# Theta's weights loaded between the first head pairs, values in 128-row transfers, later float64 weights split by Prelu

## The chip, the cores and the metric

The kernel runs on one core of one Trainium2 chip. The metric is the time of one execution in microseconds (us). The core's engines are TensorE (PE in the profile; PEld is its weight load), VectorE (DVE), ScalarE (ACT), GpSimd (POOL), and SyncE (SP), which issues nearly all of the transfers.

## The reference

Three stages follow each other, for 4 batches of 576 positions: an attention with 8 heads of 64 (heads 0 to 3 look back over a window of 32, heads 4 to 7 over 32 positions with a step of 4), a mixing layer whose angles are `theta`, and a gated layer. Cut to its core:

```python
# attention: q, k, v are (4, 8, 576, 64)
scores = np.where(masks, scale * q @ k.T, -1e9)
attn = exp(scores - max); attn = attn / (sum + 1e-9)
x = attn @ v                                  # -> (4, 576, 512)
# mixing
theta = x @ w_theta                           # 512 x 512
zr, zi = x * cos(theta), x * sin(theta)
u = x + w_tok_r @ zr + w_tok_i @ zi           # over the positions, 576 x 576
x = u + relu(u @ w_ch)
# gated layer
h = relu(x @ w_in); u, v = h[..., :512], h[..., 512:]
v_s = w_spatial @ norm(v) + b_spatial
out = (u * v_s) @ w_out
```

`w_theta`, `w_tok_r`, `w_tok_i`, `w_ch`, `w_in` and `w_out` come as float64, all other inputs as float32.

## The kernel before

Every product behind the attention is done three times, with each factor split into a high part that fits TensorE's float32r and a low rest: high by high, low by high, high by low (L367, L438, L445, L464). So each weight is split once: a copy to the high part (L146, helper `copy` at L107 to L113) and a subtraction for the low part (L147).

**Pieces of float64 weights.** A weight is loaded as pairs of 32-bit words, 128 rows by 256 or 288 columns at a time; here this is called a piece. `bits64` (L117) makes float32 of it: the high word is scaled (L131 on ACT or L133 on POOL, which shifts its exponent to where float32 has it), the low word is shifted on DVE (L134), and two more DVE instructions put the two together (L135, L136). The piece then goes through `copy` and the subtraction. Which engines do the copy, the subtraction and the scaling is given by strings: `TOK_ENG` for the token weights (the two halves of their columns), `CH_ENG`, `IN_ENG`, `OUT_ENG`, and `THETA_ENG`; their letters are the engine of the high copy, of the subtraction and of the scaling (v DVE, g POOL, a ACT; without a third letter POOL). There are 8 pieces of `w_theta` (`wth` in the profile), 9 of each half of `w_tok` (`w`), 8 of `w_ch`, 16 of `w_in` and 8 of `w_out`. The landing buffers of later pieces are four (`w64`, L123), as are those of the scaled words (`w64g`, L127), so the fifth piece is loaded when the first has been read.

**The head of the program.** `attention(0)` (L517) runs batch 0: four head pairs of three groups each, twelve groups `m`. A group is scores on PE (`s`, L258, with the mask added by L253), a maximum on DVE, three exponentials on ACT (L274), a sum and a reciprocal on DVE (L275, L276), a product on POOL (`sm`, L277); two groups later transposes (`pt`, L287) and four later the product with the values (`ps_x`, L301, L305), whose results ACT copies into `x`. All loads of batch 0 are issued at its start (`att_load`): keys `kt`, queries `qz`, values `vt`, the values of a pair behind the next pair's keys and queries. The values are 96 rows (`KW`) of 4,608 bytes for each head pair.

**Theta's weights.** `w_theta_job` is called at group `TH_FROM + TH_RATE * i // 10`, so at groups 6, 6, 7, 7, 8, 9, 9, 10, and what it issues, its load included, stands behind the softmax of that group. The token weights' first half (`tok0`) stands behind the last group's softmax.

**Theta's stage.** `th_run(0, (4, 0, 1, 2, 3))` works on five units of 128 positions (unit 4 has 64): `xh` on ACT (L359), `xl` on DVE (L362), twelve matmuls on PE (`ps_th`, L367), then on ACT `ta` (L375), an absolute value (L381) and two Sines (L384, L385), with a subtraction on DVE between (L376). Products with the transposed `x` give `zz` or `spare` (L388 to L396), which are split into `zh` and `zl` (L111, L113, L339). The token sums `ps_y` (L438, L445) take the `z` tiles in the order 8, 0, 4, 1, 5, 2, 6, 3, 7, with batch 1's attention between.

The order on each engine is the scheduler's: within what the dependencies and `issue_after` allow, it orders the instructions by its own estimate of time.

```python
w_theta_job(k, c)   # L162: load, scaling, three DVE instructions, copy and subtraction on POOL
spread(th_run(0, (4, 0, 1, 2, 3)), (jobs([lambda k=k: tok0(k) for k in K_ALL]), 2.0))
```

## Time and profile before

| | |
|---|---|
| Median of 3 runs | 549.74 us (546.46 to 550.3) |
| The profiled execution | 546.96 us, span 545.1 us |
| PE busy in the span | 526.1 us (96%) |
| DVE busy | 315.0 us (58%) |
| ACT busy | 246.7 us (45%) |
| POOL busy | 261.6 us (48%) |
| PE's part of the chain that ended last | 76% |

The span runs from the first to the last instruction of the profiled execution. A busy share is an average over stages with different limits; a stage is read from its own stretch. PE's matmuls are pipelined and overlap, so its busy time counts the union of their spans.

### The profile page before, as it was taken

To read this page: it belongs to the slowest core of one execution; us is meant where nothing else is said; L and a number is where in the kernel's file an instruction comes from. 1 tells how busy PE (TensorE), PEld (TensorE's weight loads), DVE (VectorE), ACT (ScalarE), POOL (GpSimd) and SP (SyncE) were. 2 spreads that over 40 slices of the span, in tenths; PEclk is the share of its full clock that TensorE was granted. 3 is DMA by queue.
4 is the path that set the end of the run, shared out by engine and by line. 5 is a ranking of instruction groups with operands and counts; after the bars stand their busy time and mean duration, and the time that the engine had idled before them with its cause. 6 is when DMAs were issued, how large, how long until landed. Compare 5 with 4: busy or idle time off the path is not lost.

```text
span 545.1 us, 10626 instructions
## 1 busy us (share of the span) xinstructions
PE 526.1 (96%) x3860; PEld 482.4 (88%) x3860; DVE 315.0 (58%) x830; ACT 246.7 (45%) x722; POOL 261.6 (48%) x336
## 2 busy tenths in 40 slices
PE   5987999999999999999999999999999999999997
PEld 5864889988999989998889999999899889988996
DVE  2688999899778378653882145795503057253020
ACT  4949766625656444872551125543322233233221
POOL 3484896554995259720296338355303114322040
PEclk9989899999999999999999999999999999999999
...
GB/s 205 294 88 109 234 180 191 198 193 64 141 215 228 125 182 103 209 91 1 1 1 253 365 199 275 1 158 95 49 29 174 58 40 1 0 2 77 1 1 96
DMA packets 60972, 67.19 MB, mean 123 GB/s; under 512 B 23028, under 2 KB 45816, under 8 KB 60920
## 3 DMA queue, kind: packets, MB, share of 16 engines
...
q10 hardware_dynamic: 2224, 0.55, 0.5%
...
## 4 chain that ended last, share of the span: by engine, by line
PE 76%; DVE 9%; POOL 5%; issue 4%; ACT 3%; DMA 2%; ACTq 0%; POOLq 0%; DVEq 0%
PE ps_y L445 17%; PE ps_sp L725 9%; PE ps_hu L706 9%; PE ps_o L754 9%; PE ps_hv L661 9%; PE s L258 5%; PE ps_r L464 5%; PE ps_th L367 3%; PE pt L287 3%; PE ps_x L301 2%; POOL zl L339 2%; DVE xl L362 1%; PE ps_x L305 1%; PE ps_y L438 1%; DMA x2d<-parts 1%
## 5 line engine op out<-in xcount | busy, mean ns | idle before, releaser
L445 PE MATMUL ps_y<-wtok_h,zh 128*128 128x288 f32 x270 | 81.2, 304 | 1.1 <-DVE sm L270 0.7
L445 PE MATMUL ps_y<-wtok_h,zl 128*128 128x288 f32 x270 | 80.0, 298 | 0.7 <-POOL zl L339 0.7
L445 PE MATMUL ps_y<-wtok_l,zh 128*128 128x288 f32 x270 | 79.5, 298 | 0.0
L339 POOL TENSOR_TENSOR gl<-hu,gh 128x288 fp32r<-128x288 f32 x32 | 26.1, 815 | 64.5 <-ACT gh L109 64.5
L445 PEld LDWEIGHTS ps_y<-wtok_h,zh 128*128 128x128 f32 x270 | 50.4, 188 | 2.5 <-DVE sm L270 1.4
L445 PEld LDWEIGHTS ps_y<-wtok_h,zl 128*128 128x128 f32 x270 | 50.7, 188 | 1.0 <-POOL zl L339 0.9
L445 PEld LDWEIGHTS ps_y<-wtok_l,zh 128*128 128x128 f32 x270 | 50.4, 188 | 0.3
L729 DVE TENSOR_TENSOR hu<-ps_sp,hu 128x288 f32<-128x288 f32 x32 | 14.6, 455 | 61.8 <-PE ps_sp L728 61.7
L277 POOL TENSOR_TENSOR sm<-sm,l 128x288 f32<-128x288 f32 x48 | 31.9, 669 | 34.7 <-DVE l L276 19.5
L339 POOL TENSOR_TENSOR vl<-hv,vh 128x512 fp32r<-128x512 f32 x16 | 21.1, 1319 | 56.5 <-ACT vh L109 51.5
L274 ACT ACTIVATE sm<-sm,m 128x96 f32<-128x96 f32 x108 | 39.2, 365 | 10.1 <-DVE m L271 7.2
L448 DVE TENSOR_TENSOR x<-ps_y,x 128x288 f32<-128x288 f32 x40 | 17.6, 452 | 38.2 <-PE ps_y L445 37.8
L339 POOL TENSOR_TENSOR ul<-x,uh 128x288 fp32r<-128x288 f32 x32 | 26.8, 845 | 26.0 <-ACT uh L109 23.7
L725 PE MATMUL ps_sp<-wsp_h,vh 128*128 128x288 f32 x128 | 37.8, 296 | 0.0
L464 PE MATMUL ps_r<-uh,wch_h 128*128 128x288 f32 x128 | 37.6, 298 | 0.2 <-DVE x L448 0.2
L725 PE MATMUL ps_sp<-wsp_h,vl 128*128 128x288 f32 x128 | 37.7, 295 | 0.0
L725 PE MATMUL ps_sp<-wsp_l,vh 128*128 128x288 f32 x128 | 37.7, 295 | 0.0
L464 PE MATMUL ps_r<-uh,wch_l 128*128 128x288 f32 x128 | 37.7, 296 | 0.0
L706 PE MATMUL ps_hu<-x2l,win_h 128*128 128x288 f32 x128 | 37.7, 295 | 0.0
L706 PE MATMUL ps_hu<-x2h,win_h 128*128 128x288 f32 x128 | 37.7, 294 | 0.0
L706 PE MATMUL ps_hu<-x2h,win_l 128*128 128x288 f32 x128 | 37.7, 294 | 0.0
L464 PE MATMUL ps_r<-ul,wch_h 128*128 128x288 f32 x128 | 36.9, 295 | 0.0
...
## 6 DMA issues: line engine op xcount, KB each, us to landing
...
```

What stands on the lines that cost most here:

```text
L258: PE.matmul(s[:, KW * blk:KW * (blk + 1)], qz[:, t].rearrange("p j q -> p (j q)"), kt[:, T * t:T * t + KW], start=not on_pe, stop=not on_pe)
L274: ia = A.activation(sm[:, t, :], src[:, t, :], AF.Exp, bias=m_[:, t:t + 1], scale=scale, accum_out=ls[:, t, 0:1])
L277: ig = G.tensor_tensor(sm, sm, l.unsqueeze(2).to_broadcast([P, 3, KW]), op=ALU.mult)
L287: PE.transpose(pt[:KW, P * t:P * (t + 1)], sm[:, t, :], ident)
L339: return (G if el == "g" else V).tensor_tensor(dst_l, src, f32(dst_h), op=ALU.subtract)
L445: PE.matmul(ps[:, :CH], lh[b, k][:, P * d:P * (d + 1)], rh[:, k, cs], start=(n == 0), stop=(n == 3 * len(ks) - 1))
L448: V.tensor_tensor(xv, ps[:, :CH], xv, op=ALU.add)
L464: PE.matmul(ps[:, :CH], lh[:, k, P * e:P * (e + 1)], rh[:, k, cs], start=(n == 0), stop=(n == 11))
L661: PE.matmul(ps, lh[:, k, ts_], rh[:, k, DM:], start=(n == 0), stop=(n == 11))
L706: PE.matmul(ps[:, :CH], lh[:, k, fs], rh[:, k, cs], start=(n == 0), stop=(n == 11))
L725: PE.matmul(ps[:, :CH], lh[b, k][:, fs], rh[:, k, cs], start=(n == 0), stop=False)
L754: PE.matmul(ps, lh[:, k, ts_], rh[:, k, cs], start=(n == 0), stop=(n == 11))
```

## The change

Five things are changed.

1. Theta's weights are loaded by `w_theta_load` out of `att_load`: two of the eight transfers behind the values of each head pair, ahead of the next pair's keys and queries. `w_theta_job` keeps the rest.
2. The splitting of theta's eight pieces stands behind the softmax of groups 2, 3, 4, 5, 6, 7, 8 and 9.
3. Values are loaded as 128 rows: the 96 rows of a head pair and the 32 that follow them in memory (the matmuls use the first 96), 589,824 bytes instead of 442,368. The last head pair of all has no rows behind it and keeps 96.
4. Pieces that ACT scales use Prelu with a slope of 2^32 on the negative side, which leaves the sign where the last combining instruction would have put it: two DVE instructions instead of three. That holds for the token, channel, input and output weights; theta's pieces keep three.
5. The scaling of the second half of the token weights and of `w_in` goes from POOL to ACT: 9 + 16 = 25 pieces.

```diff
-TH_FROM, TH_RATE = 6, 6
+TH_FROM = (2, 3, 4, 5, 6, 7, 8, 9)
-IN_ENG, SP_ENG, OUT_ENG = "vgg", "ag", "aga"
-TOK_ENG = ("aga", "gv")
+IN_ENG, SP_ENG, OUT_ENG = "vga", "ag", "aga"
+TOK_ENG = ("aga", "gva")
...
-        last_dma[0] = SY.dma_start(st[:p, :2 * n], src.bitcast(U32))
+        if src is not None:
+            last_dma[0] = SY.dma_start(st[:p, :2 * n], src.bitcast(U32))
...
         if eng == "a":
-            A.mul(g, hw.bitcast(F32), 2.0**-112)
-        else:
-            G.tensor_scalar(g, hw.bitcast(F32), 2.0**-56, 2.0**-56, op0=ALU.mult, op1=ALU.mult)
+            A.activation(g, hw.bitcast(F32), AF.Prelu, scale=2.0**-112, alpha=2.0**32)
+            V.tensor_scalar(c, lw, 29, None, op0=ALU.logical_shift_right)
+            V.scalar_tensor_tensor(gi, gi, 3, c, op0=ALU.logical_shift_left, op1=ALU.bitwise_or)
+            return g
+        G.tensor_scalar(g, hw.bitcast(F32), 2.0**-56, 2.0**-56, op0=ALU.mult, op1=ALU.mult)
         V.tensor_scalar(c, lw, 29, None, op0=ALU.logical_shift_right)
         V.scalar_tensor_tensor(c, gi, 3, c, op0=ALU.logical_shift_left, op1=ALU.bitwise_or)
         V.scalar_tensor_tensor(gi, gi, 0x80000000, c, op0=ALU.bitwise_and, op1=ALU.bitwise_or)
...
+    def w_theta_load(k, c):
+        wth[k, c] = pz.tile([P, DM], U32, tag=f"z{'hl'[c]}{k}", name="wth64")
+        SY.dma_start(wth[k, c], w_theta[:, k, DM // 2 * c:DM // 2 * (c + 1)].bitcast(U32))
...
+    def load_v(vt, b, hp):
+
+        r = KW * (4 * b + hp)
+        n = min(P, KW * 4 * B - r)
+        SY.dma_start(vt[:n], v_rows[r:r + n])
...
         if hp:
-            SY.dma_start(heads[0, hp - 1][2], vw[0, hp - 1])
+            load_v(heads[0, hp - 1][2], 0, hp - 1)
+            for c in range(2):
+                w_theta_load(hp - 1, c)
         if hp == 3:
-            SY.dma_start(vt, vw[0, 3])
+            load_v(vt, 0, 3)
+            for c in range(2):
+                w_theta_load(3, c)
...
-            if m == TH_FROM + TH_RATE * i // 10:
+            if m == TH_FROM[i]:
```

In the built programs the change also moves instructions. The line numbers of the changed kernel are higher; its L297, L136, L150, L132, L379, L382, L395, L396, L408 and L415 are L277, L133, L147, L131, L359, L362, L375, L376, L388 and L395 of the kernel before.

POOL, at the end of batch 0's attention, before. `sm` is the softmax product, here those of the last two groups; the others split theta's weights:

```order
L277 TENSOR_TENSOR sm<-sm,l 128x288
L133 TENSOR_SCALAR w64g<-wth_416 128x256
L147 TENSOR_TENSOR wth_l<-w64g,wth_h 128x256
L113 TENSOR_SCALAR wth_h<-w64g 128x256
L277 TENSOR_TENSOR sm<-sm,l 128x288
L133 TENSOR_SCALAR w64g<-wth_456 128x256
L147 TENSOR_TENSOR wth_l<-w64g,wth_h 128x256
L113 TENSOR_SCALAR wth_h<-w64g 128x256 x2
L133 TENSOR_SCALAR w64g<-wth_465 128x256
L147 TENSOR_TENSOR wth_l<-w64g,wth_h 128x256 x2
L113 TENSOR_SCALAR wth_h<-w64g 128x256
L133 TENSOR_SCALAR w64g<-wth_497 128x256
```

Nine theta instructions stand behind the last `sm` in these rows, and five more follow them before the first subtraction of a token piece. In the changed kernel the same place reads:

```order
L297 TENSOR_TENSOR sm<-sm,l 128x288
L150 TENSOR_TENSOR wth_l<-w64g,wth_h 128x256
L136 TENSOR_SCALAR w64g<-wth_160 128x256
L113 TENSOR_SCALAR wth_h<-w64g 128x256
L136 TENSOR_SCALAR w64g<-wth_162 128x256
L297 TENSOR_TENSOR sm<-sm,l 128x288
L150 TENSOR_TENSOR wth_l<-w64g,wth_h 128x256
L113 TENSOR_SCALAR wth_h<-w64g 128x256
L150 TENSOR_TENSOR wth_l<-w64g,wth_h 128x256
L113 TENSOR_SCALAR wth_h<-w64g 128x256
L150 TENSOR_TENSOR wth_l<-w64g,wth_h 128x256
L150 TENSOR_TENSOR wtok_l<-w64g,wtok_h 128x288 x9
```

Now five theta instructions stand behind the last `sm`, and all nine subtractions of the token weights' first half follow as a block; behind that block come the first `zl`.

ACT, at the start of theta's stage, before: the first two `xh` are those of units 4 and 0, the two that follow those of units 1 and 2; `w64g<-w` is the scaling of a token piece and `wtok_h` its high copy:

```order
L359 ACTIVATE xh<-x_148 128x4x64
L359 ACTIVATE xh<-x_148 128x512
L131 ACTIVATE w64g<-w_625 128x288
L131 ACTIVATE w64g<-w_634 128x288
L131 ACTIVATE w64g<-w_681 128x288
L131 ACTIVATE w64g<-w_690 128x288
L109 CAST wtok_h<-w64g 128x288
L375 ACTIVATE ta<-ps_th,magic 64x512
L359 ACTIVATE xh<-x_148 128x512
L375 ACTIVATE spare<-ps_th,magic 128x512
L359 ACTIVATE xh<-x_148 128x512
```

In the changed kernel three scalings and a cast already stand ahead of these rows, between the last copies into `x`:

```order
L132 ACTIVATE w64g<-w_687 128x288
L379 ACTIVATE xh<-x_164 128x4x64
L379 ACTIVATE xh<-x_164 128x512
L109 CAST wtok_h<-w64g 128x288
L132 ACTIVATE w64g<-w_732 128x288
L109 CAST wtok_h<-w64g 128x288
L132 ACTIVATE w64g<-w_740 128x288
L109 CAST wtok_h<-w64g 128x288
L132 ACTIVATE w64g<-w_787 128x288
L109 CAST wtok_h<-w64g 128x288
L132 ACTIVATE w64g<-w_795 128x288
L395 ACTIVATE ta<-ps_th,magic 64x512
```

Eight scalings instead of four stand ahead of unit 4's `ta` now, and four copies instead of one stand between the second `xh` and it.

DVE, where unit 3's `xl` stands, before: `zz` are unit 4's products, `spare` those of units 0 and 1, and the row with `ps_th` is unit 1's subtraction:

```order
L395 TENSOR_TENSOR zz<-ps_xn,tb 64x512
L396 TENSOR_TENSOR zz<-ps_xn,ta 64x512
L136 SCALAR_TENSOR_TENSOR w64g<-w64g,c_100 128x288
L388 TENSOR_TENSOR spare<-ps_xn,spare 128x512 x2
L134 TENSOR_SCALAR c_100<-w_736 128x288
L376 SCALAR_TENSOR_TENSOR spare<-spare,ps_th 128x512
L111 CAST zh_672<-spare 128x512
L362 SCALAR_TENSOR_TENSOR xl<-x_148,xh 128x512
```

And in the changed kernel:

```order
L415 TENSOR_TENSOR zz<-ps_xn,tb 64x512
L416 TENSOR_TENSOR zz<-ps_xn,ta 64x512
L396 SCALAR_TENSOR_TENSOR spare<-spare,ps_th 128x512
L382 SCALAR_TENSOR_TENSOR xl<-x_164,xh 128x512
L408 TENSOR_TENSOR spare<-ps_xn,spare 128x512 x2
L111 CAST zh_670<-spare 128x512
```

Unit 3's `xl` moved ahead of unit 0's products and cast, and no piece of the token weights stands there any more. On PE the twelve matmuls of unit 4 stood between those of unit 0; now they stand in a block, but for one. The number of ACT's table loads is nine in both programs.

## Rows read from the trace of the kernel before

**Rows 1.** Stretches (us from the start): length, busy time and instructions by engine, granted clock, DMA.

```profile
core 0: us, PE busy (x) PEld busy (x) DVE busy (x) ACT busy (x) POOL busy (x), PEclk, DMA share, GB/s
28.10:34.46 6.36, 4.11 (x60) 3.17 (x59) 5.33 (x15) 3.73 (x12) 6.36 (x14) 0.86 0.38 138
42.29:50.40 8.11, 6.21 (x25) 4.43 (x24) 6.40 (x13) 8.08 (x15) 1.91 (x2) 1.00 0.39 112
50.40:59.50 9.10, 6.16 (x23) 4.62 (x24) 9.07 (x16) 7.38 (x15) 7.88 (x8) 0.84 0.66 172
59.50:290.00 230.50, 228.05 (x1905) 210.54 (x1904) 173.80 (x450) 126.31 (x396) 143.38 (x186) 1.00 0.47 135
```

**Rows 2.** Waits of PE: for whom, us in total, times, longest.

```profile
PE ps_th L367 <- ACT xh L359: 2.4, 3, 1.1
PE ps_th L367 <- DVE xl L362: 2.4, 2, 2.1
PE pt L287 <- POOL sm L277: 2.2, 2, 1.6
```

**Rows 3.** Stretches in which values, then theta's and token pieces move.

```profile
19.50:22.00 2.50, 2.50 (x25) 2.45 (x25) 2.10 (x7) 2.34 (x13) 0.67 (x1) 1.00 1.00 237
...
24.40:29.00 4.60, 4.09 (x62) 2.79 (x60) 4.50 (x16) 4.15 (x20) 4.40 (x10) 1.00 1.06 389
```

**Rows 4.** Timeline: start us, duration us, engine, line, instruction; pair 3.

```profile
10.44 0.43 SPq L216 DMA_DIRECT2D kt<-kT  x1
...
22.44 0.21 ACT L267 ACTIVATE m<-m 128x3 f32<-128x3 f32 x1
```

**Rows 5.** Tile `kt` to 62 us: duration min/median/max, first and last start; landing.

```profile
L258 PE MATMUL s<-kt,qz_2wch_l x18: 246/275/275, 20.5 to 24.5; 128*128 128x96 f32 x18
...
DMA to landing us min/median/max: 2.2/3.7/7.3
```

**Rows 6.** Timeline of POOL.

```profile
30.92 0.67 POOL L277 TENSOR_TENSOR sm<-sm,l 128x288 f32<-128x288 f32 x1
...
40.21 0.74 POOL L147 TENSOR_TENSOR wth_l<-w64g,wth_h 128x256 fp32r<-128x256 f32 x1
...
71.16 1.27 POOL L339 TENSOR_TENSOR zl<-tb,zh 128x512 fp32r<-128x512 f32 x1
```

**Rows 7.** Groups of ACT, 34 to 64 us: busy us, mean ns, idle before.

```profile
L131 ACT ACTIVATE w64g<-w 128x288 f32<-128x288 f32 x9 | 4.1, 455 | 4.3 <-POOL wth_l L147 4.3
...
L385 ACT ACTIVATE spare<-spare,half_pi 128x512 f32<-128x512 f32 x2 | 1.4, 708 | 0.0
```

**Rows 8.** Timeline of DVE, `xl` of units 4 and 3.

```profile
34.91 2.00 DVE L362 SCALAR_TENSOR_TENSOR xl<-x,xh 128x256 fp32r<-128x256 f32 x1 [1.00 <-ACT xh L359]
...
54.11 1.27 DVE L362 SCALAR_TENSOR_TENSOR xl<-x,xh 128x512 fp32r<-128x512 f32 x1
```

**Rows 9.** The chain that ended last: start us, us, what.

```profile
36.97 5.29 PE ps_th L367 x22
...
55.44 4.10 PE ps_th L367 x11
```

**Rows 10.** Tile `w` to 62 us: time from issue to landing.

```profile
DMA to landing us min/median/max: 2.7/5.5/7.5
```

**Rows 11.** Timeline of ACT: `ta` of unit 4, `xh` of unit 3.

```profile
42.29 0.68 ACT L375 ACTIVATE ta<-ps_th,magic 64x512 f32<-64x512 f32 x1 [0.52 <-PE ps_th L367]
...
51.16 0.62 ACT L359 ACTIVATE xh<-x 128x512 fp32r<-128x512 f32 x1
```

**Rows 12.** Groups of POOL, 50 to 73 us.

```profile
L339 POOL TENSOR_TENSOR zl<-ta,zh 128x512 fp32r<-128x512 f32 x2 | 2.6, 1314 | 0.1
...
L113 POOL TENSOR_SCALAR zh<-spare 128x512 fp32r<-128x512 f32 x2 | 1.2, 612 | 0.5 <-DVE spare L388 0.5
```

**Rows 13.** Groups of DVE over the whole span.

```profile
L135 DVE SCALAR_TENSOR_TENSOR c<-w64g,c 128x256 uint32<-128x256 uint32 (+1 forms) x58 | 25.1, 433 | 3.4 <-POOL w64g L133 1.9
```

**Rows 14.** Waits between 100 and 150 us.

```profile
ACT w64g L131 <- DMA w<-w_ch: 3.8, 2, 1.9
```

More of the change, by code (lines that the diff above doesn't have):

```diff
@@ L117, in bits64 @@
     def bits64(src, n, eng, st=None):
-        p = src.shape[0]
+        p = P if src is None else src.shape[0]
         if st is None:
             st = const.tile([P, 2 * CH], U32, tag="w64", name="w64", bufs=4)
-        last_dma[0] = SY.dma_start(st[:p, :2 * n], src.bitcast(U32))
+        if src is not None:
+            last_dma[0] = SY.dma_start(st[:p, :2 * n], src.bitcast(U32))
         w = st[:p, :2 * n].rearrange("p (n w) -> p n w", w=2)
@@ L140, in split_weight @@
         n = hi.shape[-1]
-        if src.dtype == F32:
+        if src is not None and src.dtype == F32:
             s = const.tile([P, CH], F32, tag="stage", name="stage", bufs=4)[:src.shape[0], :n]
@@ L160, in stored @@
         SY.dma_start(f32(dst[:, k, :, cs]), f32(t))
+    wth = {}
+    def w_theta_load(k, c):
+        wth[k, c] = pz.tile([P, DM], U32, tag=f"z{'hl'[c]}{k}", name="wth64")
+        SY.dma_start(wth[k, c], w_theta[:, k, DM // 2 * c:DM // 2 * (c + 1)].bitcast(U32))
     def w_theta_job(k, c):
         cs = slice(DM // 2 * c, DM // 2 * (c + 1))
-        split_weight(w_theta[:, k, cs], wth_h[:, k, cs], wth_l[:, k, cs], *THETA_ENG, st=pz.tile([P, DM], U32, tag=f"z{'hl'[c]}{k}", name="wth64"))
+        split_weight(None, wth_h[:, k, cs], wth_l[:, k, cs], *THETA_ENG, st=wth[k, c])
     def w_tok_job(k, c):
@@ L187, in tile_block @@
     vt_2 = p1.tile([P, 2, NT, P], F32, tag="uh", name="vt_2")
+    v_rows = vw.rearrange("b h k t p -> (b h k) t p")
     qz_2 = [p1.tile([P, NT, 2, T], F32, tag=n, name=f"qz_2{n}") for n in ("wch_h", "wch_l")]
@@ L218, in att_load @@
                 SY.dma_start(qz[D * j:D * (j + 1), :, j], qT[b, hp, D * j:D * (j + 1)].rearrange("d (t q) -> d t q", q=T))
-        vt = vt_2[:KW, hp - 2] if early else patt.tile([KW, NT, P], F32, tag="v", name="vt", bufs=2)
+        vt = vt_2[:, hp - 2] if early else patt.tile([P, NT, P], F32, tag="v", name="vt", bufs=2)
         heads[b, hp] = (qz, kt, vt, {})
         if b:
-            SY.dma_start(vt, vw[b, hp])
+            load_v(vt, b, hp)
             return
@@ L300, in att_values @@
                 for j in range(2):
-                    values[m] = PE.matmul(ps[T * j:T * (j + 1), T * t:T * (t + 1)], vt[:, t, T * j:T * (j + 1)], pT[t // 3][:, P * (t % 3) + T * j:P * (t % 3) + T * (j + 1)], start=True, stop=True)
+                    values[m] = PE.matmul(ps[T * j:T * (j + 1), T * t:T * (t + 1)], vt[:KW, t, T * j:T * (j + 1)], pT[t // 3][:, P * (t % 3) + T * j:P * (t % 3) + T * (j + 1)], start=True, stop=True)
         else:
@@ L304, in att_values @@
                 for j in range(2):
-                    values[m] = PE.matmul(ps[T * j:T * (j + 1), T * t:T * (t + 1)], vt[:, NA + t, T * j:T * (j + 1)], pT[2][:, P * t + T * j:P * t + T * (j + 1)], start=True, stop=True)
+                    values[m] = PE.matmul(ps[T * j:T * (j + 1), T * t:T * (t + 1)], vt[:KW, NA + t, T * j:T * (j + 1)], pT[2][:, P * t + T * j:P * t + T * (j + 1)], start=True, stop=True)
         n0, n1 = (0, NA * T) if g == 1 else (NA * T, S)
```

## The prediction

> **What bounds the kernel now.** I read first the table of stretches [rows 1]: in each row PE's busy time against the stretch's length shows where PE stands still, and an engine whose busy time fills the stretch is the one to suspect. From 28.10 to 34.46 us PE is busy 4.11 of 6.36 us and POOL all 6.36; from 42.29 to 50.40 PE 6.21 of 8.11 and ACT 8.08; from 50.40 to 59.50 PE 6.16 of 9.10 and DVE 9.07, with PE's granted clock at a mean of 0.84, so part of it at the lower level (1.2 GHz). From 59.50 to 290 PE is busy 228.05 of 230.50 us although DVE is busy 173.80 of them. So DVE is crowded for long, but PE waits for its neighbours almost only before 59.5 us. PE's waits [rows 2] say the same of the head: `xh` 2.4, `xl` 2.4 and `sm` 2.2 us. The idle time of the three stretches is 2.25 + 1.90 + 2.94 = 7.1 us and the lower clock costs (1 - 0.84) x 9.10 = 1.5 us: a change in the head can give back about 8.6 us and no more.
>
> **The loads.** Pair 2's keys and queries now stand behind two of theta's transfers, pair 3's behind four (262,144 bytes each). While such 128-row transfers move the rate is 389 GB/s; while the 96-row values move it is 237 GB/s [rows 3]. Four cost 4 x 0.67 = 2.7 us ahead of pair 3, two 1.35 us ahead of pair 2. The trace has no 128-row values. The nearest rows give 589,824 bytes at 389 GB/s = 1.5 us or, at the rate seen while values moved, 2.5 us; before it is 442,368 bytes at 237 GB/s = 1.9 us. I take 1.5: they fill as many partitions as theta's transfers, which have 389. So pair 2 comes 1.35 - 0.4 = 1.0 us later and pair 3 2.7 - 0.8 = 1.9 us later (at the other bound 2.0 and 3.9). Pair 3's keys land at most 7.3 us after their issue at 10.44, its two query halves of 147,456 bytes 1.2 us behind them, near 18.9 [rows 4, 5]; PE first uses them at 20.5, and ACT starts on that pair's softmax at 22.44. With 1.9 us more they land near 20.8, and scores and reduction still fit ahead of ACT. Cost 0.2 us, at the other bound 2.2.
> The Trainium skill speaks against my price ("SBUF — State Buffer", section "Door 1: The DMA port swizzle"): by its port table a tile of 96 rows already puts eight partitions on half of the ports, as one of 128 does on all, so the longer transfer would take as long as the short one, and no less. By that rule pair 3 comes 2.7 us later and the sum is worse by 0.5 us; no row of the trace before has both forms to decide it.
>
> **Theta's split leaves the tail of attention.** POOL's last softmax product `sm` starts at 30.92, and the last piece of theta's weights is ready at 40.21 + 0.74 = 40.95 [rows 6]. Now that `sm` stands ahead of five of POOL's theta instructions and can start behind its reciprocal, about 1.2 us earlier (the theta subtraction and copy between them are gone). The gain does not reach `xh`: ACT now has three `w64g` (0.455 us each [rows 7]) and a cast in its way, 1.4 us at their pitch. So unit 4's `xh` stays where it is. But the weights are complete at 30.4 + 3.0 = 33.4 (five instructions, three of them like the one at 40.21).
>
> **Theta's stage, step by step.** Unit 4's `xl` starts at 34.91 and takes 2.00 us [rows 8], while POOL subtracts; with POOL's theta work over I take 0.7, and 0.7 for unit 0's, which ends at 36.3. The chain has 22 of PE's theta matmuls in 5.29 us, 0.24 each [rows 9]. Unit 4's twelve now stand in a block: 35.6 + 11 x 0.24 = 38.2. ACT reaches unit 4's `ta` only behind the eighth piece's `w64g`; that piece's buffer is free when DVE has shifted the fourth, at 36.3 + 0.4, and its transfer takes at least 2.7 us [rows 10]: 39.4, plus 0.455 = 39.9. Before, `ta` started at 42.29 [rows 11]: 2.4 us won.
> From there to unit 3's `xh` ACT takes 51.16 - 42.29 = 8.9 us, sixteen instructions. The new order has fourteen: the two Sines of unit 0 (up to 0.708 each [rows 7]) now stand behind it, so 7.6 us, and I add 0.5 for a cast that waits for DVE: `xh` at 48.0 instead of 51.16. Before, `xl` of unit 3 waits for DVE until 54.11 and takes 1.27 us [rows 8], because two products, a shift, a subtraction and a cast stand ahead; now only unit 1's subtraction does: 48.6 to 49.3. Theta's last matmuls end at 49.3 + 11 x 0.24 = 52.0 instead of 55.44 + 4.10 = 59.54 [rows 9]: 7.5 us earlier.
> The token sums need `zh` and `zl`, whose last ends at 71.16 + 1.27 = 72.43 [rows 6]. Now POOL has all nine `wtok_l` ahead of the first `zl`, and that waits for ACT's cast, five instructions behind unit 3's `xh`: 48.0 + 2.6 = 50.6. Then POOL needs 1.31 us for unit 4 and 0.61 + 2 x 1.31 = 3.2 for each of four units [rows 12]: 64.9, 7.5 us earlier. PE has 78 token matmuls of 288 columns in those 13 us (0.135 each by theta's 512 columns, 10.5 us) and 28 score matmuls, so it keeps pace.
> Two things take some of it back. Batch 1's first softmax products queue behind those `zl` on POOL, and PE's transposes wait for two of them, 0.7 us. And the stretch of lower clock, which fell on theta's matmuls, would fall on token sums that partly wait for `zl` anyway: between 0 and 1.5 us, I take 0.5. Head: 7.5 - 0.2 - 0.7 - 0.5 = 6.1 us. The bounds are 8.6 (all idle time gone) and 0 (each wait replaced).
>
> **The later pieces.** Fifty pieces lose one DVE instruction of 0.433 us [rows 13], 21.7 us in all; PE's busy time covers it. Behind 59.5 only 230.50 - 228.05 = 2.4 us of idle PE can be won; without that cover it would be all 21.7. I take 0.7, bounds 0 and 2.4. Prelu is not in the trace; its neighbours on ACT are the scaling it replaces, 0.455, and the Sine, at most 0.708 for nearly twice the columns [rows 7]. The new combining instruction differs from the old one of 0.433 only in where it writes. Both at no more than before. Twenty-five scalings go from POOL to ACT, 25 x 0.455 = 11.4 us; ACT is busy 126.31 of 230.50 us there [rows 1], which covers them while their transfers are in time. The twelve later value transfers carry a third more bytes; the DMA share there is 0.47, which covers them.
>
> **Sum.** 6.1 + 0.7 = 6.8 us. The profiled execution took 546.96 us (span 545.1), so 540.2. The median of the runs shown is 549.74, 2.8 above it, with runs from 546.46 up; from the median it is 542.9. I forecast between the two: 541.5 us.
>
> **Rivals.**
> *Half of it.* POOL or ACT keeps PE waiting in the head. For it: each fills one of the three stretches. Against it: theta's work leaves the stretch in which POOL is full. If `zl` comes only 3 us earlier, because POOL's and DVE's subtractions slow one another as in the `xl` of 2.00 us, the head gives 2.5 us, in all about 3: 545.5. The port rule and the slow bound of the values end on this side too (6.8 - 0.5 and 6.8 - 2.0).
> *No effect.* DVE's relief lies off the path, as PE's share behind 59.5 says, and the head's waits only change their names: 548.5, the middle of the two starting points. It counts with the half.
> *More.* The stretch of lower clock goes as PE idles less, and the later waits go: 6.8 + 1.0 + 1.7 + 0.7 for the softmax products: 10, so 538.
> *Slower: scalings block ACT.* ACT already waited 3.8 us for two pieces of `w_ch`, 1.9 each [rows 14]. The 25 moved scalings stand in one queue with the exponentials of batches 1 and 2; if each waits like that it is 47 us of ACT. The gain is gone once 6.8 us of it reach PE, about four such waits that the softmax does not absorb; with seven, 13.3 us, the time is 555. Against it: ACT has idle time of 104 us there.
>
> **Chances.** Forecast (a gain of 4 to 9.5 us) 0.55, half or nothing (0 to 4) 0.27, more 0.09, slower 0.09. About 1% (5.5 us) is what a measurement of this kernel can tell from no change. Nearly four fifths of the forecast lie beyond it (0.43), with the larger gain 0.52; slower by over 1% needs the ACT rival in its strong form, 0.06; the rest, 0.42, is within 1%. The range holds 8 in 10: from 535 (the larger gain from the lowest run) to 549.5 (no gain). The forecast's own range is 537 to 546.
>
> **What the profile would show.** Theta's last subtraction on POOL near 33 us rather than 41; unit 4's `ta` near 40; theta's last matmul near 52; the last `zl` of batch 0 near 65; PE's waits for `xh` and `xl` under 2.5 us together. Values of 128 rows at over 350 GB/s confirm the price of the loads, near 316 (589,824 bytes in the 1.87 us of before) the port rule. I am wrong if unit 4's `ta` stays at 42 or later (ACT waits for the eighth piece), if the last `zl` ends later than 69, or if `w64g` shows long waits for `w` behind 60 us while PE waits for `sm`.

## The result, and the profile after

The changed kernel takes 542.97 us (median of 7 runs, 541.75 to 544.14); before, over the runs beside it, 548.72. The ratio is 0.9912 with a 95% interval of 0.9895 to 0.9929: 0.88% faster, some 4.8 us (3.9 to 5.8); the two medians by themselves are 5.75 us apart. The gain is just under the 1% that I had named as the bound of "within 1%", and clear of no change. The profiled execution took 543.24 us (span 541.5), 3.7 us less than that of before.

| | before | after |
|---|---|---|
| PE busy | 526.1 us | 523.0 us |
| DVE busy | 315.0 us | 299.0 us |
| ACT busy | 246.7 us | 250.9 us |
| POOL busy | 261.6 us | 251.5 us |

The stretches of [rows 1] in the changed kernel, with 34.46 to 42.29 us in each kernel beside them (columns as in [rows 1]; line numbers below are those of the kernel shown). After:

```profile
28.10:34.46 6.36, 3.83 (x49) 2.92 (x51) 5.27 (x17) 3.84 (x15) 6.19 (x13) 0.71 0.34 125
34.46:42.29 7.83, 7.83 (x47) 5.94 (x44) 5.79 (x13) 6.35 (x18) 4.89 (x6) 0.80 0.62 171
42.29:50.40 8.11, 7.00 (x29) 4.87 (x27) 5.74 (x11) 7.35 (x14) 3.04 (x3) 1.00 1.08 299
50.40:59.50 9.10, 8.68 (x59) 7.74 (x58) 8.33 (x15) 9.04 (x18) 7.47 (x7) 1.00 0.49 143
59.50:290.00 230.50, 226.54 (x1899) 209.71 (x1898) 161.02 (x410) 128.59 (x410) 132.35 (x160) 1.00 0.46 137
```

And before, the one that [rows 1] left out:

```profile
34.46:42.29 7.83, 7.48 (x34) 5.41 (x32) 6.84 (x12) 3.01 (x8) 4.91 (x10) 0.89 0.12 35
```

Three things are to be seen. PE is hardly idle any more between 50.40 and 59.50 us (8.68 of 9.10 us busy, 6.16 before). Its lower clock has only moved: before it cost (1 - 0.86) x 6.36 + (1 - 0.89) x 7.83 + (1 - 0.84) x 9.10 = 3.2 us, now 0.29 x 6.36 + 0.20 x 7.83 = 3.4 us, all of it ahead of 42.29. And behind 59.50 PE is idle for 3.96 us, where it was 2.45, although DVE is busy for 12.8 us less there.

The lower clock cost the two profiled executions about the same, so it does not make the 3.7 us between them. Over the runs it may have a part: the mean granted clock was 0.994 of full speed in the changed kernel's seven, and 0.990 to 0.991 in the four sets of runs of the kernel before that were taken beside the experiments. How much of the 4.8 us that is, no run tells.

The steps of the prediction in the timeline of the changed kernel (start us, us, engine, line, instruction): the last softmax product, theta's last subtraction, theta's first matmul, unit 4's `ta`, unit 3's `xh`, theta's last matmul, the last `zl` of batch 0.

```profile
31.44 0.67 POOL L297 TENSOR_TENSOR sm<-sm,l 128x288 f32<-128x288 f32 x1
...
34.43 0.73 POOL L150 TENSOR_TENSOR wth_l<-w64g,wth_h 128x256 fp32r<-128x256 f32 x1
...
37.57 0.71 PE L387 MATMUL ps_th<-wth_h,xh 128*64 128x512 f32 x2
...
41.88 0.67 ACT L395 ACTIVATE ta<-ps_th,magic 64x512 f32<-64x512 f32 x1
...
50.43 0.62 ACT L379 ACTIVATE xh<-x 128x512 fp32r<-128x512 f32 x1
...
54.31 0.40 PE L387 MATMUL ps_th<-wth_l,xh 128*128 128x512 f32 x1
...
66.17 1.28 POOL L359 TENSOR_TENSOR zl<-ta,zh 128x512 fp32r<-128x512 f32 x1
```

Theta starts 1.4 us later than before (37.57, was 36.15) and takes 17.1 us instead of 23.4, so it ends 4.8 us earlier (54.71, was 59.54). PE's waits over the whole span (total, times, longest) answer to [rows 2]: no `xh` stands among them any more, `xl` has 1.4 for 2.4, and `sm` has 3.3 for 2.2. (The third row is a wait near 203 us, which comes up below.)

```profile
PE pt L307 <- POOL sm L297: 3.3, 2, 1.9
PE ps_th L387 <- DVE xl L382: 1.4, 3, 0.7
PE ps_r L484 <- DVE ta L396: 1.0, 1, 1.0
```

Why it starts later is in the chain of the changed kernel (start, us, what): the transfers of pairs 2 and 3 are its two longest pieces ahead of theta. Pair 2's keys land at 9.29 + 6.12 = 15.4 us (13.45 before) and pair 3's queries at 15.43 + 7.78 = 23.2, and PE uses the queries at once.

```profile
9.29 6.12 DMA kt<-kT
15.43 7.78 DMA qz_2wch_l<-qT
...
23.34 0.88 PE s L278 x6
...
39.68 4.36 DMA w<-w_tok
...
44.12 0.46 ACT w64g L132
```

**The lead, point by point.** To see where the time comes from and goes, I take the same matmul in both traces, counted in the order of the program, and call the difference of its times the lead. It is 4.8 us at theta's last matmul, 5.5 at batch 0's first channel product (`ps_r`, 109.48 us before), 6.3 at batch 1's (186.41), and 3.7 at the 172nd of the 228 theta matmuls (256.06) and from there to the end. So the head gives 4.8 us, batch 1 adds 1.5, and 2.6 us go again between 180 and 252 us.

### The profile page after: what moved, and what is told of

The parts are those of the page before. It is cut to its first block, busy times and chain, and to the rows that moved or that the text cites. A ratio compares the mean times of both kernels' runs of the same rounds, so it can differ in the third digit from the quotient of the medians.

```text
span 541.5 us, 10544 instructions
## 1 busy us (share of the span) xinstructions
PE 523.0 (97%) x3860; PEld 480.5 (89%) x3860; DVE 299.0 (55%) x784; ACT 250.9 (46%) x743; POOL 251.5 (46%) x311
## 4 chain that ended last, share of the span: by engine, by line
PE 83%; DMA 6%; DVE 4%; ACT 3%; POOL 2%; issue 1%; SPq 0%; ACTq 0%; DVEq 0%; POOLq 0%
PE ps_y L465 19%; PE ps_sp L745 9%; PE ps_hu L726 9%; PE ps_o L774 9%; PE ps_hv L681 9%; PE ps_r L484 8%; PE ps_th L387 6%; PE s L278 4%; PE pt L307 3%; PE ps_x L321 2%; DMA qz_2wch_l<-qT 1%; PE ps_x L325 1%; DMA kt<-kT 1%; PE ps_xn L399 1%; DMA w<-w_tok 1%
## 5 line engine op out<-in xcount | busy, mean ns | idle before, releaser
L465 PE MATMUL ps_y<-wtok_l,zh 128*128 128x288 f32 x270 | 80.6, 299 | 0.0
L359 POOL TENSOR_TENSOR gl<-hu,gh 128x288 fp32r<-128x288 f32 x32 | 25.9, 813 | 66.8 <-ACT gh L109 66.8
L297 POOL TENSOR_TENSOR sm<-sm,l 128x288 f32<-128x288 f32 x48 | 32.5, 678 | 36.0 <-DVE l L296 24.7
L359 POOL TENSOR_TENSOR vl<-hv,vh 128x512 fp32r<-128x512 f32 x16 | 21.0, 1317 | 56.7 <-ACT vh L109 51.6
L294 ACT ACTIVATE sm<-sm,m 128x96 f32<-128x96 f32 x108 | 39.2, 364 | 12.7 <-DVE m L291 7.5
L359 POOL TENSOR_TENSOR ul<-x,uh 128x288 fp32r<-128x288 f32 x32 | 26.6, 840 | 28.0 <-ACT uh L109 28.0
```

The costliest lines, as they stand in the source:

```text
L294: ia = A.activation(sm[:, t, :], src[:, t, :], AF.Exp, bias=m_[:, t:t + 1], scale=scale, accum_out=ls[:, t, 0:1])
L297: ig = G.tensor_tensor(sm, sm, l.unsqueeze(2).to_broadcast([P, 3, KW]), op=ALU.mult)
L359: return (G if el == "g" else V).tensor_tensor(dst_l, src, f32(dst_h), op=ALU.subtract)
L465: PE.matmul(ps[:, :CH], lh[b, k][:, P * d:P * (d + 1)], rh[:, k, cs], start=(n == 0), stop=(n == 3 * len(ks) - 1))
```

## The experiments

The five parts are numbered as in the change. Each kernel was timed beside the kernel before on its own chip. Its lead comes from its one profiled execution, at the five points just named (theta's end; the first channel product of batch 0; of batch 1; the 172nd theta matmul, that is the third and fourth batch; the last matmul).

| kernel | parts | median us | ratio (95%) | lead at the five points |
|---|---|---|---|---|
| changed | 1 2 3 4 5 | 542.97 | 0.9912 (0.9895, 0.9929) | 4.8, 5.5, 6.3, 3.7, 3.7 |
| e1 | 1 2 | 546.97 | 0.9985 (0.9965, 1.0005) | 1.7, 1.6, -2.2, -2.2, -2.2 |
| e2 | 3 4 5 | 546.61 | 0.9984 (0.9965, 1.0003) | -1.9, 0.3, 0.7, -1.8, -1.8 |
| e3 | 1 2 3 4 | 544.09 | 0.9932 (0.9911, 0.9952) | 5.3, 4.6, 3.0, 3.1, 3.1 |
| e4 | 1 2 3 5 | 545.03 | 0.9948 (0.9929, 0.9968) | 6.4, 5.6, 5.3, 2.5, 2.5 |
| e5 | 1 2 4 5 | 548.89 | 1.0013 (0.9985, 1.0041) | 1.1, 1.4, 0.4, -1.9, -1.9 |
| e6 | 1 2 3 4, of 5 only `w_tok` | 541.03 | 0.9865 (0.9836, 0.9893) | 4.5, 5.0, 5.6, 5.7, 5.7 |
| e7 | 1 2 3 5, 4 not for `tok0` | 543.45 | 0.9907 (0.9874, 0.9939) | 4.3, 6.1, 6.3, 3.4, 3.4 |
| e8 | e7, of 5 only `w_tok` | 541.19 | 0.9872 (0.9843, 0.9902) | 6.6, 8.2, 5.8, 5.8, 5.8 |
| e9 | 1 2 3 | 547.21 | 0.9987 (0.9972, 1.0001) | 5.8, 4.3, -0.7, -0.6, -0.6 |
| e10 | e6, fewer loads ahead of pair 3 | 543.98 | 0.9936 (0.9912, 0.9961) | 3.5, 4.7, 4.8, 4.9, 4.9 |
| e11 | 1 2 3, of 5 only `w_tok` | 543.80 | 0.9925 (0.9902, 0.9948) | 6.7, 5.9, 4.3, 4.3, 4.3 |
| e12 | e10 with `tok0` as in e7 | 541.59 | 0.9878 (0.9853, 0.9903) | 0.1, 1.7, 2.0, 2.1, 2.1 |

The profiled executions of e1, e2 and e12 were among the longest of their kernels (549.11 of 544.06 to 550.27; 549.12 of 545.37 to 549.25; 544.85 of 541.08 to 544.85), so for these three the end of the lead is 2 to 3 us under what the median says. A lead is one execution of each kernel and has no interval; what the parts are worth is read from the ratios.

### Theta's parts alone, and without them

Each is the changed kernel with the other parts undone. For e1:

```diff
-IN_ENG, SP_ENG, OUT_ENG = "vga", "ag", "aga"
-TOK_ENG = ("aga", "gva")
+IN_ENG, SP_ENG, OUT_ENG = "vgg", "ag", "aga"
+TOK_ENG = ("aga", "gv")
...
-            A.activation(g, hw.bitcast(F32), AF.Prelu, scale=2.0**-112, alpha=2.0**32)
+            A.mul(g, hw.bitcast(F32), 2.0**-112)
...
-        n = min(P, KW * 4 * B - r)
+        n = KW
```

> The kernel before with parts 1 and 2 alone (theta's loads between the head pairs, its splitting behind groups 2 to 9); values in 96 rows, three VectorE instructions a piece, scalings where they were. Theory T (theta's earlier split carries the gain): theta's last matmul ends at 54 to 56 us (59.54 before, about 54.7 in the changed kernel) and the time is 4 to 6 us below that of before, 543 to 545. Rival D (the VectorE instruction that nine token pieces lose inside theta's stage, 9 x 0.433 = 3.9 us, carries it): theta's last matmul ends at 57.5 or later and the gain is under 2.5 us.

For e2, with the load out of `att_load` and back at the head of `w_theta_job`:

```diff
-TH_FROM = (2, 3, 4, 5, 6, 7, 8, 9)
+TH_FROM = (6, 6, 7, 7, 8, 9, 9, 10)
...
         cs = slice(DM // 2 * c, DM // 2 * (c + 1))
+        w_theta_load(k, c)
...
-            for c in range(2):
-                w_theta_load(hp - 1, c)
...
```

> The changed kernel with parts 1 and 2 undone: theta's loads stand behind the last values again and its splitting behind groups 6, 6, 7, 7, 8, 9, 9 and 10. Theory T: theta's last matmul ends at 58 us or later and the gain over before is 0 to 2 us. Rival D: it ends at 56 or earlier and 3 to 5 us of the gain stay.

Measured: 0.15% and 0.16%, neither clear of nothing. For e2 that is what theory T had said; for e1 it is a miss, and it fell where rival D had put it (theta's end at 57.79). D fails in e2, though, where theta ends at 61.41 and not by 56, and again in e4 below. Parts that give 0.15% and 0.16% apart and 0.88% together need each other, which no step of the prediction has. One caution: e2 keeps the scaling of `w_in` on ACT, which costs some 0.47% (shown below), so its parts without that may be worth more than 0.16%. PE's waits in e1 show one half of why:

```profile
PE s L276 <- DMA qz_2wch_l<-qT: 1.9, 1, 1.9
...
PE s L276 <- DMA qz<-qT: 1.3, 1, 1.3
PE s L276 <- DMA qz_2wch_h<-qT: 1.1, 1, 1.1
```

PE stands 4.3 us for queries, and theta starts at 40.18. That the 96-row values alone do this is not shown: in e5 below, with the same loads, PE waits 0.8 us for queries. What the ends of theta say is that the 128-row values help the head: theta ends 4.0 us earlier with them in e9 than in e1, and 3.7 us earlier in the changed kernel than in e5. The other half comes behind: the lead of 1.7 us at theta's end is -2.2 at batch 1.

### Parts 5 and 4 undone

e3 has the two strings of engines as in the diff of e1, and nothing else of it; e4 has its second piece:

```diff
-            A.activation(g, hw.bitcast(F32), AF.Prelu, scale=2.0**-112, alpha=2.0**32)
-            V.tensor_scalar(c, lw, 29, None, op0=ALU.logical_shift_right)
-            V.scalar_tensor_tensor(gi, gi, 3, c, op0=ALU.logical_shift_left, op1=ALU.bitwise_or)
-            return g
-        G.tensor_scalar(g, hw.bitcast(F32), 2.0**-56, 2.0**-56, op0=ALU.mult, op1=ALU.mult)
+            A.mul(g, hw.bitcast(F32), 2.0**-112)
+        else:
+            G.tensor_scalar(g, hw.bitcast(F32), 2.0**-56, 2.0**-56, op0=ALU.mult, op1=ALU.mult)
```

> The changed kernel with part 5 undone: the 25 scalings stand on POOL again, and with them these 25 pieces have three VectorE instructions. The changed kernel is 6.5 us ahead of before at 125 us and 3.9 at 240; the 2.6 us go between 200 and 240. If the moved scalings take them (ACT reaches theta's copies of batch 2 later), this kernel keeps its 6 us to the end and is 1.5 to 2.5 us faster than the changed one, 540.5 to 541.5. If they come from the order that the scheduler chose there, or from the pieces of w_in on the other engines, it is within 1 us of the changed one, 542 to 544.

> The changed kernel with part 4 undone: ACT scales with a product, and VectorE has three instructions for each piece, 50 more in all (21.7 us). Theory T with PE as the cover of the later pieces: 0 to 2 us slower than the changed kernel, 543 to 545, and at 59.5 us it is at most 1 us behind it. Rival D: theta's stage is longer by 2 to 4 us, theta's last matmul ends at 57 to 59, and the time is 546 or more.

e3 took 544.09 and e4 545.03. In e3 the loss behind 180 us is gone, but 1.6 us of its lead go earlier, between batch 0 and batch 1, and its time is a hair above both ranges that I had given. e4 is slower than the changed kernel by 2 us, at the end of what theory T allowed, and yet its lead at theta's end is larger, 6.4 us. Its ACT shows unit 4's `ta` at 39.73 (41.88 in the changed kernel), behind an `xh` at 35.57 (36.52):

```profile
35.57 0.94 ACT L377 ACTIVATE xh<-x 128x256 fp32r<-128x256 f32 x2
...
39.73 0.68 ACT L393 ACTIVATE ta<-ps_th,magic 64x512 f32<-64x512 f32 x1
```

With three instructions a piece the scheduler puts six scalings and three casts ahead of that `ta`, with Prelu eight and five. From `xh` to `ta` it is 4.2 us here and 5.4 there: the order that comes with Prelu costs theta's stage up to 1.2 us. In e7, e8, e9 and e11, which have six and three as well, it is 4.6 to 5.2 us, since `ta` there waits 0.4 to 1.0 us for PE.

### Values in 96 rows

```diff
-        n = min(P, KW * 4 * B - r)
+        n = KW
```

> The changed kernel with part 3 undone: values in 96-row transfers, all else as changed. Theory V (the longer value transfers are what makes room for theta's between the pairs): pair 3's keys land at 23.5 to 24.5 us (21.08 in the changed kernel, 24.13 with parts 1 and 2 alone), the first theta matmul starts at 39.5 to 40.5 (37.57 in the changed kernel), and the time is 2 to 4 us above the changed kernel's, 545 to 547. Rival P (a 96-row transfer costs what a 128-row one costs; the loss of parts 1 and 2 alone lies in VectorE's three instructions): pair 3's keys land at 20.5 to 21.5 and the time is that of the changed kernel within 1 us, 542 to 544.

548.89, no gain at all; pair 3's keys land at 21.52, as rival P had it, theta starts at 38.25, earlier than theory V had it, and the time is above both. What the transfer itself costs is plain where values move between theta's pieces (the same stretch in the changed kernel, then in e5):

```profile
25.60:28.60 3.00, 1.78 (x33) 1.45 (x31) 2.65 (x11) 3.00 (x18) 1.36 (x3) 1.00 1.05 392
```

```profile
25.60:28.60 3.00, 2.54 (x45) 1.95 (x45) 2.20 (x8) 2.66 (x17) 1.43 (x3) 1.00 1.02 248
```

392 GB/s with 128 rows and 248 with 96. In the changed kernel a pair's first theta piece lands at 25.11, its second, the last values and one more theta piece follow until 27.91: 2.80 us, less two pieces of 0.67 us leaves 1.46 us for 589,824 bytes. In e5 the same runs from 26.34 to 29.81: 2.13 us for 442,368 bytes. The longer transfer is the shorter one in time; e1 has 1.98 us for its 96 rows by the same sum, and the seven other kernels with the changed kernel's loads 1.42 to 1.49 for 128. In e5 theta's last piece lands at 30.50 (28.58 in the changed kernel), and the scheduler also puts ACT's table load and two Sines ahead of unit 0's theta result; unit 2's `xh`, behind that, comes at 47.86 instead of 45.91, and PE stands 1.8 us for it. PE's granted clock, 1.00 in the changed kernel from 50 to 54 us, is 0.72 there. How much of the 1.0% between the two kernels is transfer, how much order and how much clock can't be told apart here.

### Where the lead goes behind 180 us

```diff
-IN_ENG, SP_ENG, OUT_ENG = "vga", "ag", "aga"
+IN_ENG, SP_ENG, OUT_ENG = "vgg", "ag", "aga"
```

> The changed kernel with part 5 undone for w_in alone (16 pieces scaled on POOL with three VectorE instructions each); the token weights' second half stays with ACT. If the w_in pieces with ACT's scaling take the 2.6 us that the changed kernel loses between 200 and 240 us, this one keeps its lead of about 6 us: 539.5 to 541.5, and PE has no wait of over 0.5 us for VectorE's subtraction near 200. If the token half does it, or the schedule in general, it loses there as well and comes to 542.5 to 544.

541.03, a ratio of 0.9865: the lead stays (5.6 at batch 1, 5.7 at the end). The column of leads says the same of all kernels: the five with `w_in` scaled on ACT (changed, e2, e4, e5, e7) lose 2.3 to 2.9 us between the third and the fourth point, the other eight lose nothing there. e8 against e7, the same step with another token order, gives 0.35%. The rows of the changed kernel at that place, POOL first, then DVE, ACT and PE (in brackets the idle time before and its releaser):

```profile
197.32 1.54 POOL L359 TENSOR_TENSOR zl<-ta,zh 128x512 fp32r<-128x512 f32 x1
198.81 1.35 POOL L359 TENSOR_TENSOR zl<-tb,zh 128x512 fp32r<-128x512 f32 x1
...
197.62 1.39 DVE L111 CAST parts<-w64g 128x256 fp32r<-128x256 f32 x1
198.93 1.52 DVE L403 TENSOR_SCALAR tb<-ta 128x512 uint32<-128x512 uint32 x1
...
200.48 0.63 ACT L404 ACTIVATE ta<-ta 128x512 f32<-128x512 f32 x1 [4.77 <-DVE tb L403]
...
203.69 0.40 PE L484 MATMUL ps_r<-uh,wch_h 128*128 128x288 f32 x1 [1.00 <-DVE ta L396]
```

The cast of a `w_in` piece takes 1.39 us and the absolute value behind it 1.52; in e6 the same two take 0.38 and 0.42:

```profile
197.87 0.42 DVE L403 TENSOR_SCALAR tb<-ta 128x512 uint32<-128x512 uint32 x1
...
198.53 0.38 DVE L111 CAST parts<-w64g 128x256 fp32r<-128x256 f32 x1
```

In the changed kernel each starts 0.1 to 0.3 us behind a `zl` of POOL and ends 0.15 and 0.29 us behind its end (198.86 and 200.16). The same pair, 1.38 to 1.39 and 1.50 to 1.52 us, stands near this place in the traces of all five kernels with `w_in` scaled on ACT; in the others no such cast there takes over 0.65 us and no such absolute value over 0.63. ACT waits 4.77 us for that absolute value, and PE 1.0 us for the subtraction that follows. The Trainium skill has the rule ("SBUF — State Buffer", section "Who interferes with whom"): VectorE's casts and scalar operations in their fast modes and GpSimd's instructions want one pair of ports, and the later one is held for the whole of the other. The trace agrees in the main, with the ends just given; but these lie less behind POOL's than the 0.38 and 0.42 us that the two take in e6, so they were not held to the very end. That the pieces on ACT bring these four together is the scheduler's order; that the order, and not ACT's load, costs the time is argued from these rows, and no run keeps the one and changes the other. Of the 2.6 us, 1.9 go between 203 and 206 us of the changed kernel, behind these rows; the other 0.7 goes later, and why stays open.

### The token weights' first half with three instructions

A letter for ACT's product with three DVE instructions:

```diff
-TOK_ENG = ("aga", "gva")
+TOK_ENG = ("agA", "gva")
...
+        if eng == "A":
+            A.mul(g, hw.bitcast(F32), 2.0**-112)
+        else:
+            G.tensor_scalar(g, hw.bitcast(F32), 2.0**-56, 2.0**-56, op0=ALU.mult, op1=ALU.mult)
```

> The changed kernel with three VectorE instructions and a product on ACT for the nine pieces of the token weights' first half alone; Prelu for all others. With three instructions for all pieces unit 4's first theta result left PE at 39.73 us instead of 41.88 and theta's last matmul ended at 53.14 instead of 54.71, although VectorE had more to do. If that is the order that the nine pieces take on ACT (fewer casts and scalings ahead of that result), it is seen here too: 39.5 to 40.3, theta's end at 52.8 to 53.6, and 0.5 to 1.5 us below the changed kernel, 541.5 to 542.5. If it came from elsewhere, theta ends at 54.4 or later and the time is the changed kernel's, 543.

> Both of the two before: three VectorE instructions for the token weights' first half, and w_in scaled on POOL. If the head's gain (5.8 us at 60 us with three instructions) and the loss between 200 and 240 us are separate things, the gains add: 539 to 541, the fastest of all. If the lead cannot outlast the crowded stages of batch 1 and 2 whatever the engines do, it ends at 542 to 544 as the others do.

e7 took 543.45: no gain over the changed kernel, as the second branch had it. Its `ta` comes at 40.53, but its theta ends at 55.28, since PE waits 1.2 us for an `xl` near 49 us and its clock has a mean of 0.57 from 51 to 55. e8, whose head has the same order, ended theta at 52.98 in its profiled execution, and took 541.19, no less than e6 and a hair above the range for gains that add. So 2 us of lead at theta's end (6.6 for 4.5) are worth nothing at the end (5.8 for 5.7): what e8 has more, batch 1 takes.

### Parts 1 to 3, and nine scalings

e9 is the changed kernel with both of e1's first pieces and the 128-row values kept.

> The kernel before with parts 1, 2 and 3 alone: theta's loads between the pairs, its earlier split, 128-row values; three VectorE instructions for every piece and the scalings where they were. Parts 1 and 2 alone gave 0.15%, parts 3 to 5 alone 0.16%, all five 0.88%, all but the scaling of w_in on ACT 1.35%. Theory V (theta's split and the 128-row values need each other, the rest adds little): theta's last matmul ends at 53 to 55 us, the lead at 60 us is 4 to 6 us and the time 542 to 544.5. If the shorter chain of VectorE is needed as well, theta ends at 56 or later and the time is 545 to 547.

e11 differs from it in nine instructions that move from POOL to ACT:

```diff
-TOK_ENG = ("aga", "gv")
+TOK_ENG = ("aga", "gva")
```

> Parts 1 to 3 and, of part 5, the nine scalings of the token weights' second half on ACT; no Prelu, w_in scaled on POOL. With parts 1 to 3 alone the lead of 5.3 us at about 83 us was gone by 175 us, VectorE being busy 19.0 of 20 us between 110 and 130. Theory B (behind the head the pieces' chain on POOL and VectorE stands close behind TensorE, and relief there is what keeps the lead): nine POOL instructions fewer between 60 and 80 us, where POOL is busy 19.2 of 20 us, let VectorE take the pieces earlier, the lead stays at 4 us or more at 175 us, and the time is 541.5 to 544. If Prelu's shorter chain on VectorE is what keeps it, the lead falls under 2 us again and the time is 545.5 to 547.5.

e9: theta ends at 53.77, as theory V had it, and the time is 547.21, a hair above what the other had for the time: the lead of 5.8 us is -0.7 at batch 1. e11: 543.80, as theory B had it. The stretches 60 to 80, 110 to 130 and 130 to 150 us (columns as in [rows 1], DVE's busy time the third), e9 first, then e11, and 110 to 130 us of the kernel before:

```profile
60.00:80.00 20.00, 19.42 (x179) 18.77 (x179) 16.16 (x47) 12.15 (x51) 19.20 (x28) 1.00 0.43 118
...
110.00:130.00 20.00, 19.29 (x99) 15.33 (x97) 19.02 (x44) 9.02 (x15) 7.99 (x12) 1.00 0.46 149
130.00:150.00 20.00, 17.68 (x126) 17.32 (x125) 16.77 (x34) 12.63 (x30) 18.19 (x20) 0.92 0.41 117
```

```profile
60.00:80.00 20.00, 19.42 (x176) 18.47 (x176) 19.78 (x58) 15.31 (x61) 17.51 (x24) 1.00 0.64 171
...
110.00:130.00 20.00, 19.62 (x105) 15.82 (x103) 16.98 (x35) 9.12 (x15) 7.23 (x9) 1.00 0.36 113
130.00:150.00 20.00, 18.86 (x145) 18.15 (x144) 15.20 (x39) 11.45 (x36) 18.89 (x22) 1.00 0.41 125
```

```profile
110.00:130.00 20.00, 19.65 (x115) 16.58 (x114) 19.12 (x42) 6.90 (x14) 9.62 (x12) 1.00 0.53 169
```

In e9 POOL is full between 60 and 80 us (19.20 of 20), seven scalings among its work, while DVE has 3.84 us free; between 110 and 130 DVE is busy for 19.02 of 20 us, and behind that PE stands still: 2.3 us for DVE and a stretch at the lower clock (0.92). In the kernel before DVE was as full (19.12), but PE, later by the lead, stood for it only 0.5 us there. With the nine scalings off POOL, DVE is busy for 19.78 us early and 16.98 late, and PE keeps its lead. How far DVE has come by 80 us shows in the last step of a token piece that it does itself (groups of DVE, 60 to 80 us; e9, then e11): three pieces are done in the one, six in the other.

```profile
L148 DVE TENSOR_TENSOR wtok_l<-w64g,wtok_h 128x288 fp32r<-128x288 f32 x3 | 1.8, 600 | 0.0
```

```profile
L148 DVE TENSOR_TENSOR wtok_l<-w64g,wtok_h 128x288 fp32r<-128x288 f32 x6 | 3.8, 638 | 0.0
```

### Fewer of theta's transfers ahead of pair 3

Both stand on e6; e12 adds e7's letter for the token weights' first half.

```diff
-TH_FROM = (2, 3, 4, 5, 6, 7, 8, 9)
+TH_FROM = (2, 4, 6, 7, 8, 8, 9, 9)
...
-            for c in range(2):
-                w_theta_load(hp - 1, c)
+            for i in ((), (0,), (1,), (2, 3))[hp]:
+                w_theta_load(i // 2, i % 2)
...
```

> The changed kernel with w_in scaled on POOL, and only two instead of four of theta's transfers ahead of pair 3's keys (one behind the values of pair 0, one behind pair 1's, two behind pair 2's, four at the end), split behind groups 2, 4, 6, 7, 8, 8, 9 and 9. If the late keys of pair 3 cost the head about 1.4 us as the first theta matmul shows (37.57 for 36.15 before), pair 3's keys land 1 to 1.5 us earlier (near 20), theta starts near 36.5, and the time is 0.5 to 1.5 us below the 541.0 of the kernel with four ahead: 539.5 to 540.5. If theta's later pieces then hold up POOL behind the last softmax product, the first theta matmul starts at 37.5 or later and the time is 541 to 542.5.

> The kernel with two of theta's transfers ahead of pair 3's keys and w_in on POOL, and for the nine pieces of the token weights' first half three VectorE instructions instead of Prelu. That kernel started theta at 33.0 us, 4.5 us ahead of the one with four transfers, but ended it at 56.0, since unit 4's result waited on ACT behind six scalings and three casts of token pieces until 40.65. Here two casts stand ahead of it. If these are what holds it, the result leaves at 39 to 40, theta ends at 53 to 54.5, and the time is 540 to 542; if ACT waits for the landing of the pieces, theta ends at 55.5 or later and the time is 543 to 545.

In e10 theta starts at 33.02, 4.5 us ahead of e6, and ends at 56.02, 0.9 behind it; the time is 543.98, slower than e6, and its runs spread from 541.0 to 546.5. My theory that the late keys cost what they delay falls: theta starts earlier by more than I had expected, and the time is none the better. ACT shows why:

```profile
36.41 0.43 ACT L109 CAST wtok_h<-w64g 128x288 fp32r<-128x288 f32 x1 [1.47 <-DVE w64g L134]
...
38.74 0.47 ACT L132 ACTIVATE w64g<-w 128x288 f32<-128x288 f32 x1 [0.84 <-DMA w<-w_tok]
...
40.28 0.46 ACT L132 ACTIVATE w64g<-w 128x288 f32<-128x288 f32 x1 [0.76 <-DMA w<-w_tok]
40.65 0.67 ACT L395 ACTIVATE ta<-ps_th,magic 64x512 f32<-64x512 f32 x1
```

Unit 4's `ta` and the next `xh` stand in one queue behind token pieces that have to land and to pass DVE; PE waits 2.7 us for that `xh`. An earlier start is spent there. e12 took 541.59, in its range for the time and no different from e6, and 0.58% below e10; its one profiled execution was its longest, with PE's theta at 36.41 to 59.40, and tells nothing of the median. Why its runs differ by 3.8 us stays open.

## Why the prediction was right, and where it was not

The time, 541.5 forecast and 542.97 measured, its sign and its rough size were right; several steps were not, and they cancel in part, which is luck. The sum said 6.8 us; the ratio says 4.8, and the two traces 3.7. That 541.5 came so near owes something to the starting point, chosen between 540.2 and 542.9. Of the chances, the 0.42 for "within 1%" came out, and not the 0.52 for more. Forecast: head 6.1, later 0.7. Measured by the lead: head 4.8, then +1.5 in batch 1, then -2.6.

1. **Theta's stage: right in its durations, in part by luck.** I had 5.4 us from unit 4's `xh` to its `ta` (34.46 to 39.9); it is 5.4 (36.52 to 41.88). From there to unit 3's `xh` I had 8.1; it is 8.55. From that to the last theta matmul 4.0; it is 4.3. From there to the last `zl`, 12.9; it is 12.7. Waits for `xh` and `xl` together 1.4, under the 2.5 that I named. PE's idle time there went. But the first of these is right for another reason than mine. I let ACT wait for the landing of the eighth piece; the wait ahead of that piece's scaling, and one before it, is for POOL's `wtok_l` (0.88 and 0.42 us, the rows below). And my sign of being wrong, a `ta` at 42 or later, was missed by 0.12 us.
2. **The loads: mis-sized, and with it the start.** I let unit 4's `xh` "stay where it is" at 34.46 and charged 0.2 us for pair 3. The `xh` came at 36.52, 2.06 us late, and what follows is late by 2.0 to 2.7: `ta` 41.88 for 39.9, the last matmul 54.7 for 52.0, the last `zl` 67.45 for 64.9. The last `sm`, ahead of it all, started at 31.44 where I had 29.7. The price of one value transfer was right (1.5 us, measured 1.46), and what I had drawn from the Trainium skill ("SBUF — State Buffer", section "Door 1: The DMA port swizzle") was not: by it the long transfer takes as long as the short one, and it took 1.46 us for 2.13. (My price for that rule was also wrong: with the slack that gives 0.2 us at 1.9 late and 2.2 at 3.9, 2.7 late costs 1.0, so the sum would be 0.8 us worse, not 0.5.) What I missed is that transfers here do not land as sums of their prices: pair 2's keys came 2.0 us later, not 1.0, and pair 3's 3.4 (21.08 for 17.72), not 1.9. In the eight kernels with the same loads ahead of them, one execution each, pair 2's land between 14.24 and 15.98 us (13.45 before) and pair 3's between 19.50 and 22.27: my sums are near the lower ends. SyncE also issues these keys 1.65 and 2.77 us later than before (9.29 and 13.21 us, 7.64 and 10.44 before), with theta's issues ahead of them; no run tells that from the transfers themselves, and what makes the difference between the executions stays open. And the lower clock fell on the last products of the attention and the transposes, between 28 and 42 us, behind PE's waits for `sm`, not on the token sums. So theta's weights, complete at 34.43 + 0.73 = 35.16 instead of 33.4, were in time all the same.
3. **The later pieces: the step that failed.** I wrote that PE's busy time covers DVE's relief, with 0 to 2.4 us to win. That was read from a trace in which PE is the late one. Move PE 5.8 us ahead (e9) and it runs into the pieces on POOL and DVE, and nearly all of the gain goes: 0.13% is left, not clear of nothing. Nine scalings off POOL keep it (e11, 0.75%), Prelu adds to that (e6, 1.35%). So to an early PE the nine scalings are worth some 0.6%, and Prelu about as much, with them (e6 against e11) or without (e3, 0.68%, against e9). What they are worth to a late PE is not shown: e2's 0.16% has the cost of `w_in` on ACT in it, and no run has parts 3 to 5 without that. The sum held them for 0.7 us; with neither of them the head's gain is gone.
4. **Twenty-five scalings on ACT at no cost: half wrong.** The nine of the token weights are a gain. The sixteen of `w_in` cost 0.47% (e6 against the changed kernel), not by the rival's way: ACT's longest wait for a piece of `w_in` is 2.6 us and PE does not wait for it. Most of it goes behind 197 us, where DVE's short instructions meet POOL's `zl`.
5. **Prelu's price: right.** The fifty on ACT take 446 ns in the mean (455 for the scaling of [rows 7]), and DVE's two instructions 432 and 425 ns.
6. **The rivals.** "Half" would have had the `zl` 3 us earlier; it was 5.0. "Slower" needed waits that reach PE, and there were none of that kind. The range's lower end, 535, is 1.5 below what its own words give (546.46 - 10).

The two waits of item 1, on ACT:

```profile
38.89 0.47 ACT L132 ACTIVATE w64g<-w 128x288 f32<-128x288 f32 x1 [0.42 <-POOL wtok_l L150]
...
41.52 0.46 ACT L132 ACTIVATE w64g<-w 128x288 f32<-128x288 f32 x1 [0.88 <-POOL wtok_l L150]
```

Prelu's rows of item 5:

```profile
L132 ACT ACTIVATE w64g<-w 128x256 f32<-128x256 f32 (+1 forms) x50 | 21.7, 446 | 15.2 <-DMA w<-w_in 4.5 <-POOL parts L150 3.7 <-DMA w<-w_ch 2.7
...
L133 DVE TENSOR_SCALAR c<-w 128x256 uint32<-128x256 uint32 (+1 forms) x50 | 21.6, 432 | 1.8 <-DMA w<-w_in 1.1
L134 DVE SCALAR_TENSOR_TENSOR w64g<-w64g,c 128x256 uint32<-128x256 uint32 (+1 forms) x50 | 21.2, 425 | 3.1 <-ACT w64g L132 1.6
```

(The groups of ACT and DVE over the whole span of the changed kernel: busy us, mean ns, idle before.)

The kernel with the lowest median is e6, the change without the scaling of `w_in` on ACT, at 541.03 us (0.9865); e8 and e12 are no different within their intervals.
